# A top-k attention and token mixer on one core: the product's addend made by two-step instructions, scratch rows in turn, unread matmuls placed anew, and a refitted order

## The chip, the cores and the metric

The kernel runs on one core of a Trainium2 chip. The metric is the device time of one execution in microseconds (us). Five engines work side by side, each through its own list of instructions in order: PE (matrix products), DVE (maxima and small arithmetic), ACT (activations and copies out of PSUM), POOL (elementwise work), SP (which issues most transfers). The execution before takes 740.91 us (median of 3 runs, 740.88 to 741.44).

## What is computed

For 8 batches of 8 heads, 576 rows, head size 64: attention in which each row keeps only its 32 largest scores, then a token mixer and a channel mixer.

```python
scores = scale * np.matmul(q, k.transpose(0, 1, 3, 2))
kth = np.partition(scores, -top_k, axis=-1)[..., -top_k:-top_k + 1]
scores = np.where(scores >= kth, scores, -1000000000.0)
attn = softmax(scores)
x = (attn @ v).transpose(0, 2, 1, 3).reshape(B, S, H * D)
u = x + (np.maximum(x.transpose(0, 2, 1) @ w_tok1, 0.0) @ w_tok2).transpose(0, 2, 1)
out = u + np.maximum(u @ w_ch1, 0.0) @ w_ch2
```

## The kernel before

The 64 heads are 32 pairs. A pair's q, k and v are loaded and transposed, and its rows are taken 128 at a time. A *duo* is two such tiles (two heads of 128 rows, 576 scores each); there are 144 duos, in groups of one or two. For each duo:

- PE makes the scores (L552), and ACT copies them to `SX`, shifted and scaled (L367).
- DVE cuts each row into six pieces, takes the 8 largest of each (L589), and from these finds the place in the sorted row near which the 32nd value lies (L592 to L595). This gives an estimated threshold, `nh` (L684).
- ACT counts with a Sign how many scores are above the estimate (L606): the result goes to a scratch row `sg` that nobody reads, and the sum to `cnt`. From `cnt` small DVE instructions make `gs`, `ws` and `as` (all L684): whether to look above or below, and how far.
- POOL turns the scores into whole numbers that sort in the needed direction (L614, with a few fillers, L617), and DVE takes the 8 largest of the 584 (L623) into `tlo`. One of these is the exact threshold; `nt` (L684) is its negative.
- 100 duos (the *swapped* ones) then go through PE again: POOL makes a mask `U` (L632), PE adds it to the scores (L562, L568), and ACT takes the exponential into `Pm` (L637). The other 44 (the list `KEEP` and the duos that mix two pairs) do it on POOL: the addend `no` = 256 `gs` + `nt` is made on DVE (L703), POOL makes a byte mask `M` from it (L643) and multiplies the exponential `E` by it (L647).
- SP transposes `Pm` to `PT` by a transfer (L669); PE multiplies by v (L725), DVE divides by the sums into `Xb` (L739, L742).

After the four pairs of a batch come its mixers: L789 to L846 the token mixer, L911 and L897 the first channel product (`H`, and `Ht` for the last 64 rows of two batches), L863 and L868 the second, then ACT or DVE copies to `ob` (L881, L876) and SP stores.

All instructions are first put into a `Plan` with an engine, a duration and their dependences. The order in which they are issued is the string `ORDER`: two characters for each operation give its place. `Plan.run` walks through it, keeps for each engine the time at which it becomes free, and for each buffer (a `Buf`, a slot among equal tiles) when it can be taken. From these planned times follow two things: which slot or PSUM bank an operation gets, and where *unread matmuls* stand (`heat`, L1041): products of a constant that are written into a free bank and read by nobody, as many as fill eight tenths of the planned wait of PE. Nine stand at the start, 53 later.

The three copies that the small instructions write come from this helper; only the first is used, as a per-partition scalar on ACT or POOL:

```python
def thrice(x):
    return x.unsqueeze(1).to_broadcast([P, 3, x.shape[1]])
```

Of the kernel before, what the change touches and what calls it, by code (L numbers as in the profile page):

```python
# [8 lines left out]
P = 128  # L9
# [30 lines left out]
    "&1&J&Q&[&_'4&R&S'''-'7$-$0$?$S$]$@$e$A%#%+%-$;$i$<$=$|$>%&%.%>%T%E%R%S%_%`%g%s%p%q&C&e&m&p'0'2'1'3'8'q(0(2$M$U$X"  # L40
    "%$%2$b$c${%<%C%H%%%/%5%;%4%(%@%D%L$N$V$Z$a%)$g%0$}%6%I%W$_%3$~$y%7%*%?%J%Z%]%x%w%v%y&+&3&?&H&X&W&r&w&I&U&T&y'$'G"
    "'e'f'n'r(y'j(;(M(j({$j$t%,%1%A%=%a%G&'&*&6%b&-%f%d%c&%&4&7&;$W$s$z%K%~&$%'%^&,&:&=%8%X%V%[%B%M&(&2&@&B&]'.&`'*'@"
    "'<'D'g'l'h't(*'i'k'd(/(4(:(B(C(n(p(|(q(r(})E)r)w*2*4#3#2#5$.$/$C$B#R&M&L'6'(')'+',(@%O%P%e&G&9&E&>&b&f&l&q%U&A&0"
    "&5%h&D&k&u'%%N%Q%Y&h&s&z&n&i&~'>'A&#&c&<&/&8&j&{&}'E%|'H'Q'p'O'P()(~(#(+(=(?(A(^(d(>(D(E(g)$)&)7)C)D)I)U)u)L)Q)M"
    ")R)v%u%{&d&x'&&g'R'L'Y'b'x&F'='C&v&a'B'S'^($&Z&^&o'U'_&t'M'K'c'}(&&|'X'?'#']'J'a'z(((,(H(G(K(J(`(a(f)K(v(u)])c(t"
    ")P(s)e)m)o)x)y)}*V*Y)z)|*X*^*{'/';'I'Z'W'T'v'w(.(5(N'F'u(1(-(7'`(9(R(V's(](m(x)=)6)@)O){)N*0*8*>*H*O*Q*P*R*|+M+X"
    "+`':'N'y(U'|(Q(S(')#)*)-'V(h(T'[(P(%),)1)3'm'o'{(Y(3'~(Z(8(_)+)8(6)(([)%(W(O)0):)<)?)[)S)H)Z*7*;*?*J*M*L*b*i*K+$"
    "*N*y+:+=+P+Q+y+},)+N+{+~,(,x(F(I(X)_(b)a)^)`)d)p*$(c(e)h)>)4)g)k*#*)(o(w).)/)2);)j)5)q*'*,)')9)l)))b)i*%*(*/*1*T"
    "*]*S*[*z*g*r+(+)+&+>+F+'+S+%+W+c+g,$,%,+,-,w,2,3,K,p,y-9-F-H(L(i*I*U+z+|-Z-e(k(l*W*Z,,,7-h.?-i.G.A.F.B.H/Q/Y.Z/T"
    ".]/X.[.y/P/S181T171S151U1s1w1t1x2^2j2n3/3W3x4g5=5t6`5s5~6%<)'9'5-m)B)A)G)F.P&K(z&P*_*`+#*~,N)J)T*&***E*A*5*=*a*q"  # L50
    '*w)f)~*D*.)n*f*k*v+2)V)X*-*c*3*C*e*n*s+<+?*+*B*h*l*p*6*t+;+A+-+C+L+K+J+I+l,E+i+k,0,/,1,G,J,4,L,.,Q,U,X,[,s,t-$-/'
    "-j-4-8-6-T-k)W)Y*9*F*d*@*x*:+3+@+D*<*u*j*o*m*G+1+5+e+*+,+0+[+6+9+4+E+a+d+h+7+8+^+_+Z+Y+b+f+j+o,',8,6,&,T,S,],v,o"
    ',u-&-+-5-7-3-;-?-D-U-n.@.D/4-p-r.I.R/5+++.+B+s+V+w+n+u,:,<,D+U,A+t+x+m,>,B,I,P+G,^-1-#-L-A-J-q-o-s.2.9.<.a.t.v.u'
    '.w/6/[/d/h+/+H+T+r,@+],=,;,C,R,b+p,9+q+v,?,F,H,O,d,5,M,Y,_,Z,c,a,f,h,j,l,V,e,g,W,i,`,k,m,n-(-W-V-g-f.%.$./.J.Q.O'
    ".f.i.K.N.L.n/0/2/@/C/]/v04/A0'02060;,|-%-*-P-E---<-@-b-d-y-'-)-I-O-,-B-S-^-|-2-:-M-N-z-_-a-c.#.(.*-G-Q-v-`-u-R-x"
    ".'.,...V.W.C.E/'.s.|/=/>/:/G/I/?/</;/M/O/f0&0,0:0<1+0-0.0_0}1,1_1b1e,**}/7,q,r,},~0/)t,{)s.T.S.X.U1%-.-0-=->.&.5"
    '-C.1.8.l.p-K.h.7-}-{.c.k.o.{-X-Y-]-w.^.+.b.0.d.m.~-~.`.=.4.:.;.q.}/$.>/&/D/V/E/U/b0A/c/o0*0%0)0C0I0+000(0N0R0T0Z'
    "1&1N1i1m2b1(1)1'1*1/-[-t.).-.e.g.r.z/+/-/L.3/#/%.6._.j/K/N/`.Y.x/)/3/*/_/./^/g/l/t/(/1/H/,///J/n/q/x/}0512091319"
    '1:1>1K1M1L1Z1]1O1R1P1f1h1k1p1q262_2d1r282e2k2{/9/F/j/k0>/~0$/r0B0F0H/a/w/e/m/y/z/|0E0M/Z0V0^141^1C1H1`1a1Q1y1{1}'
    '2$27292;2f2m353I3M/R/W/i0D/p0#0L0Q0Y0a0i/s0K0U/{0c0[0n0x0{/u010@0k0J0j0b0h0o0r1<0?0s0q0v0p0G0|1=1A1I1u1W1V1X2U2#'  # L60
    '2,2g2h2<2r2t2i3(2:2y373=3R3S3w3{4=3Q3V3z4*4>07080O1;0P0X0W0y1?1D1F0S0t0f0z0e0m1B1G2)0=0]0`1E1c1g1[1z1~2(2-0d0g0w'
    "0l1@0u1d1|2/212l2a2`2]2u2w3'3*3,3+3;3>3)3-3.3@3D3G3T3U4)4:4?4&4'4O4X4e5>5z6.6[6a6^6d6v7;6}7T7Q7S7R7U8i8s8v8{8y8}"
    '9S9^8j8w9Q9W:*:>9R:=:+:U9U9]:,:T:d;%:c<&;2<$;1;C;F<%;>;E<#<.<3<p<t<r=-=Z@5=$=0=a=.=/=`Af/8-l2|1#0~11104$,z034h2~'
    "2}31305a161J1Y2'202.1j2+232@2L252=2D2E2O2H2S2V2X1l1n2&2?2F2A2I2N2P2W2Z2%2C2K2*2J242R2Y2v332z323O3Y3N3b3`3a3q3|3~"
    '4#40423}4(4%474F4J4N4R4S4o4p5k4U4V4T4W5l1o1v222M2>2G2q2x3<3K3[2B2T2Q2p2[2s3A3_3o2o3#3&3E3C3B393?3d3m3t3$3:3%383F'
    "3f3h3l3u4+4@4q494n5153595B5E5C5P5U5F5D5G5X5]5_5e5g6'6]6_5f6Q6c6q6r34363L3p3^4,3r434H4M4b3H3c4-3n3J464C4L4t3y5-5A"
# [1164 lines left out]
```

## Time and profile before

| what | value |
|---|---|
| median of 3 runs | 740.91 us |
| the profiled execution | 740.52 us |
| its span in the trace | 738.7 us |
| busy PE, DVE, ACT, POOL | 682.5, 675.4, 663.5, 637.4 us |
| mean granted clock of PE | 0.988 |

A row of the timeline has the start in us, the duration in us, the engine, the line, the operation, what it writes and reads, the count, and in brackets how long the engine was idle before it and for whom. Rows of groups end in busy us and mean ns of one, then the idle time ahead. Durations of successive DVE or ACT instructions overlap a little: what an instruction costs its engine is the time from its start to the next start. A window's row has its bounds and length, then busy us with counts for PE, PEld (weight loads), DVE, ACT and POOL, then the granted clock, the share of the transfer engines and GB/s.

### The profile page before, as it was taken

The page shows a single profiled execution, that of the slowest core. Times are in us where ns is not written, and L with a number is a line of the kernel's source. Part 1 is how long each engine was busy: PE and PEld are TensorE (multiplying, and loading weights), DVE is VectorE, ACT ScalarE, POOL GpSimd, SP SyncE. Part 2 cuts the span into 40 slices and gives each one's busy share as a digit, 9 for nine tenths or more (in the row PEclk, how much of TensorE's full clock was granted, in tenths as well). Part 3 has the DMA queues.
Part 4 walks back from the last instruction along what each step waited for, and adds up shares of the span by engine and source line. Part 5 has one row for each costly group of instructions (what it writes and reads, how often), then busy time and mean ns, then how long its engine had stood idle before and what let it go on. Part 6 is the DMA issues. An engine that isn't in the chain of part 4 may idle for free.

```text
span 738.7 us, 22205 instructions
## 1 busy us (share of the span) xinstructions
PE 682.5 (92%) x7478; PEld 379.1 (51%) x7478; DVE 675.4 (91%) x3768; ACT 663.5 (90%) x1134; POOL 637.4 (86%) x867
## 2 busy tenths in 40 slices
PE   7579789999998999999999999999989999999995
PEld 4235455455555555555555555554555655564652
DVE  7999999999999999999999999999999999996530
ACT  6979999999999999999899989999999999999341
POOL 3989999999889999989978999989999999999400
PEclk9879999999999999999999999999999999999998
DMA  5568798785856656874594486774676768644511
GB/s 130 99 128 150 124 164 152 144 142 83 182 94 139 134 123 97 162 145 81 106 169 111 88 135 123 175 131 95 108 148 121 151 103 121 133 74 100 129 45 61
DMA packets 286713, 90.42 MB, mean 122 GB/s; under 512 B 273024, under 2 KB 283136, under 8 KB 286592
## 3 DMA queue, kind: packets, MB, share of 16 engines
q1 hardware_dynamic: 282768, 84.97, 60.2%
q0 software_dynamic: 3024, 3.77, 3.6%
q8 instruction: 60, 0.98, 0.6%
q14 instruction: 61, 0.50, 0.2%
q10 hardware_dynamic: 800, 0.20, 0.1%
HBM read 35.85 MB, written 9.44 MB: 61 GB/s over the span
## 4 chain that ended last, share of the span: by engine, by line
DVE 49%; PE 18%; ACT 16%; POOL 10%; issue 3%; DMA 2%; SPq 0%; POOLq 0%; ACTq 0%; DVEq 0%
DVE cd L589 21%; DVE tlo L623 15%; ACT sg L606 6%; PE bank L863 4%; ACT SX L367 4%; POOL SX L614 4%; PE bank L911 3%; DVE cd L593 3%; PE bank L552 3%; POOL U L632 2%; ACT Pm L637 2%; DVE thi L595 2%; PE bank L568 2%; DVE m L592 2%; POOL Pm L647 2%
## 5 line engine op out<-in xcount | busy, mean ns | idle before, releaser
L589 DVE MAX8 cd<-SX 128x8 f32<-128x96 f32 x1728 | 342.1, 244 | 7.5 <-ACT SX L367 7.0
L614 POOL TENSOR_SCALAR SX<-SX,nh,gs 128x576 int32<-128x576 f32 x288 | 234.3, 821 | 11.6 <-DVE gs L684 3.6
L606 ACT ACTIVATE sg<-SX,nh 128x576 bf16<-128x576 f32 x288 | 223.6, 779 | 8.3 <-DVE nh L684 5.4
L623 DVE MAX8 tlo<-SX 128x8 uint32<-128x584 uint32 x288 | 218.3, 758 | 10.8 <-POOL SX L614 5.1
L552 PE MATMUL bank<-kT,qT 64*64 64x288 f32 x2304 | 175.0, 420 | 14.7 <-ACT SX L367 7.2
L632 POOL TENSOR_SCALAR U<-SX,nt,ws 128x576 uint8<-128x576 int32 x200 | 163.2, 825 | 20.9 <-DVE nt L684 8.7
L367 ACT ACTIVATE SX<-bank 128x1152 f32<-128x1152 f32 (+1 forms) x147 | 161.8, 1110 | 14.3 <-PE bank L552 12.3
L568 PE MATMUL bank<-kT,qT 64*128 64x288 f32 x800 | 124.4, 430 | 0.0
L552 PEld LDWEIGHTS bank<-kT,qT 64*64 64x64 f32 x2304 | 77.1, 134 | 91.6 <-ACT SX L367 22.3
L637 ACT ACTIVATE Pm<-bank 128x1152 bf16<-128x1152 f32 x100 | 112.8, 1131 | 8.9 <-PE bank L568 5.1
L647 POOL TENSOR_TENSOR Pm<-E,M 128x576 bf16<-128x576 bf16 x88 | 111.5, 1278 | 2.2 <-DMA PT<-Pm 0.5
L863 PE MATMUL bank<-wc2b,H 128*128 128x512 bf16 x384 | 90.9, 380 | 0.2
L911 PE MATMUL bank<-UT,wc1b 128*128 128x512 bf16 x380 | 89.6, 379 | 0.8 <-ACT SX L367 0.6
L568 PEld LDWEIGHTS bank<-kT,qT 64*128 64x128 f32 x800 | 69.1, 186 | 32.4 <-issue 22.4
L643 POOL TENSOR_SCALAR M<-SX,no,ws 128x576 int8<-128x576 int32 x88 | 72.2, 825 | 3.7 <-DVE no L703 1.9
L863 PEld LDWEIGHTS <-H 128*128 128x128 bf16 x384 | 34.6, 98 | 47.1 <-issue 12.8
L911 PEld LDWEIGHTS <-wc1b 128*128 128x128 bf16 x380 | 34.7, 98 | 45.9 <-issue 10.9
L606 ACT ACTIVATION_READ_ACCUMULATOR sg<-SX,nh 128x1 f32 x288 | 57.7, 200 | 0.0
L562 PE MATMUL bank<-U,identN 64*64 64x288 bf16 x800 | 45.1, 294 | 13.3 <-ACT SX L367 5.5
L725 PEld LDWEIGHTS <-PT 128*128 128x128 bf16 x1600 | 52.2, 98 | 9.0 <-issue 5.2
L600 ACT ACTIVATE E<-SX,lift 128x1152 bf16<-128x1152 f32 x44 | 55.4, 1260 | 0.1
L725 PE MATMUL bank<-vb,PT 128*128 128x65 bf16 x1600 | 54.4, 194 | 0.7 <-ACT SX L367 0.6
(124 smaller groups left out, 812.6 us busy)
## 6 DMA issues: line engine op xcount, KB each, us to landing
vL<-in_v_dram SPq DMA_DIRECT2D x64, 128.0 KB, 2.6
kL<-in_k_dram SPq DMA_DIRECT2D x63, 128.0 KB, 3.0
qL<-in_q_dram SPq DMA_DIRECT2D x62, 128.0 KB, 3.0
out_dram<-ob SPq DMA_DIRECT2D x14, 512.0 KB, 3.4
PT<-Pm SPq DMA_TRANSPOSE x143, 3.6
wc1b<-in_moe_w_ch_dram POOLq DMA_DIRECT2D x4, 384.0 KB, 4.8
...
```

The costliest lines, as they stand in the source:

```text
L367: nc.scalar.activation(out=dst, in_=src, func=AF.Copy, scale=GRID, bias=-LEVEL * GRID)
L552: nc.tensor.matmul(out=row(s1.t, h, lo, lo + HS, c, 64), lhsT=x["qT"].t[r, q0 : q0 + 64], rhs=x["kT"].t[r, lo : lo + HS], start=True, stop ...
L568: nc.tensor.matmul(out=row(s2.t, h, lo, lo + HS), lhsT=x["qT"].t[r, q0 : q0 + P], rhs=x["kT"].t[r, lo : lo + HS], start=False, stop=True)
L589: ss.append(plan.add("DVE", 0.06 + (bounds[a + 1] - bounds[a]) / 960, lambda a=a, h=h, cd=cd: nc.vector.max(cd.t[:, a, :], Sb.t[:, h, boun ...
L606: got.append(plan.add("ACT", 0.761, lambda i=i0 + 1 - h, h=h: nc.scalar.activation(out=sg[:, h, :], in_=Sb.t[:, h, 0:S], func=AF.Sign, sca ...
L614: xo.append(plan.add("POOL", 0.805, lambda i=i0 + 1 - h, h=h: nc.gpsimd.tensor_scalar(out=xi(Sb)[:, h, 0:S], in0=Sb.t[:, h, 0:S], scalar1= ...
L623: mxs.append(plan.add("DVE", 0.674, lambda i=i0 + 1 - h, h=h: nc.vector.max(tlo[:, at(i) - 7 : at(i) + 1], Sb.t[:, h, :].bitcast(u32)), [d ...
L632: us.append(plan.add("POOL", 0.805, lambda i=i0 + 1 - h, h=h: nc.gpsimd.tensor_scalar(out=byte(U.t[:, h, :], 1), in0=xi(Sb)[:, h, 0:S], sc ...
L637: oe = [plan.add("ACT", 1.013, lambda: nc.scalar.activation(out=Pm.t[:, :, 0:S], in_=pairs(s2.t), func=AF.Exp, scale=scale), [orr], use=[s ...
L647: oe.append(plan.add("POOL", 1.262, lambda h=h, M=M: nc.gpsimd.tensor_tensor(out=Pm.t[:, h, 0:S], in0=E.t[:, h, :], in1=M.t[:, :], op=ALU. ...
L863: nc.tensor.matmul(out=po, lhsT=H.t[:, fc, r0 : r0 + P], rhs=wc2b[:, fc, :], start=(fc == 0), stop=(rows is not None and fc == NF - 1))
L911: nc.tensor.matmul(out=o, lhsT=wc1b[:, cc, fc * P : (fc + 1) * P], rhs=UT.t[:, cc, :], start=(cc == 0), stop=(cc == (hi if whole else NC) ...
```

## The change

1. The addend `no` is made for each half of a duo by itself: 88 instructions in place of 44. Instead of one instruction with two tensor inputs over the whole group, each reads three copies of one value of `gs`, multiplies by the constant 256 and adds a value of `nt` that it gets as a pointer scalar. Each half's product on POOL waits for its own instruction.
2. The scratch row of the Sign is a slot of two that are taken in turn, and no longer the half of a fixed tile that belongs to the half of the duo.
3. Unread matmuls may go into a bank that the waiting operation itself is about to take, and are put in only where the planned start is before 80 us. 9 and 46 stand in place of 9 and 53.
4. Some planned durations are new, an SP transfer gets a surcharge when the transfers are behind, and `ORDER` is a new list with 44 more operations. (A line of it stands for all.)

```diff
 ORDER = (
-    "$I$r$o%k%o&Y&V(<+O+R,#.M/B1$###$#4#%#&#(#'#+#,#.#6#Q#*#)$(#M#K#S#O$L#-#/#0#7#1#?#8#=#<#C#A#@#E#H#J#9#;#:#F#B#D#G"
...
-    FAR = 0.09
-    LIT, FIRST = 0.5, 9
+    FAR, CLOG = 0.06, 0.25
+    WARM, LIT, FIRST = 80.0, 0.5, 9
...
-                bs = sorted((x[1], k) for k, x in enumerate(self.tags["ps"]) if x[2] and x[1] < st)
-                if bs:
+                own = [k for b in o.acq if b.tag == "ps" for k in b.slot]
+                bs = sorted((x[1], k) for k, x in enumerate(self.tags["ps"]) if (x[2] or k in own) and x[1] < st)
+                if bs and st < self.WARM:
...
-            o.end = free[o.eng] = st + o.dur
+            o.end = free[o.eng] = st + o.dur + (self.CLOG * max(0.0, dma_free - st - 2.0) if o.eng == "SP" else 0.0)
...
-    sg = sbt("sg", [P, 2, S], bf16)
+    sgs = slots("sg", 2, [P, S], bf16)
...
-                got.append(plan.add("ACT", 0.761, lambda i=i0 + 1 - h, h=h: nc.scalar.activation(
-                    out=sg[:, h, :], in_=Sb.t[:, h, 0:S], func=AF.Sign, scale=1.0, bias=nh.t[:, il - i : il - i + 1],
-                    accum_out=cnt[:, NT - 1 - i : NT - i]), [oh], use=[Sb, nh], lat=0.17))
+                sg = Buf("sg")
+                got.append(plan.add("ACT", 0.761, lambda i=i0 + 1 - h, h=h, sg=sg: nc.scalar.activation(
+                    out=sg.t[:, :], in_=Sb.t[:, h, 0:S], func=AF.Sign, scale=1.0, bias=nh.t[:, il - i : il - i + 1],
+                    accum_out=cnt[:, NT - 1 - i : NT - i]), [oh], acq=[sg], use=[Sb, nh], lat=0.17))
...
-                    ou = plan.add("POOL", 0.805, lambda i=i0 + 1 - h, h=h, M=M: nc.gpsimd.tensor_scalar(
-                        out=byte(M.t[:, :], 1).bitcast(i8), in0=xi(Sb)[:, h, 0:S], scalar1=no.t[:, il - i : il - i + 1],
+                    ou = plan.add("POOL", 0.83, lambda i=i0 + 1 - h, h=h, M=M: nc.gpsimd.tensor_scalar(
+                        out=byte(M.t[:, :], 1).bitcast(i8), in0=xi(Sb)[:, h, 0:S], scalar1=no.t[:, 3 * (il - i) : 3 * (il - i) + 1],
...
-                        [oo, ow], acq=[M], use=[Sb, no, ws])
+                        [oo[i0 + 1 - h], ow], acq=[M], use=[Sb, no, ws])
...
-            no = Buf("no")
-            oo = plan.add("DVE", 0.066 + 0.0035 * n, lambda: nc.vector.scalar_tensor_tensor(
-                out=no.t[:, 0 : 3 * n], in0=thrice(gs.t[:, 0:n]), scalar=256.0, in1=thrice(nt.t[:, 0:n]),
-                op0=ALU.mult, op1=ALU.add), [on], acq=[no], use=[gs, nt])
+            no, oo = Buf("no"), {}
+            for i in [d[0] + 1 - h for d in ds if not d[1] for h in (1, 0)]:
+                oo[i] = plan.add("DVE", 0.119, lambda i=i: nc.vector.tensor_scalar(
+                    out=no.t[:, 3 * (il - i) : 3 * (il - i) + 3], in0=thrice(gs.t[:, il - i : il - i + 1]), scalar1=256.0,
+                    scalar2=nt.t[:, il - i : il - i + 1], op0=ALU.mult, op1=ALU.add), [on],
+                    acq=[no] if len(oo) == 0 else [], use=[no, gs, nt])
```

The other edits are planned durations: transfers of q, k, v from 1.9 to 2.0, transposes from 1.36 to 1.4, stores from 0.65 to 0.7, weights' time on the transfer engines from 2.2 to 2.6, the scores' latency 0.29, and the judge at the end takes the two scratch rows by their new names.

The lists of instructions, at three places. First DVE in the middle of the program, around the 25th of the 44 addends, before (MAX of `cd` are the pieces of the next duos, `tlo` the 8 largest whole numbers of others):

```order
L684 TENSOR_SCALAR nt_163<-tlo 128x6
L589 MAX cd_103<-SX_92 128x8
L595 MAX thi<-cd_108 128x8
L589 MAX cd_107<-SX_92 128x8
L703 SCALAR_TENSOR_TENSOR no_167<-gs_135,nt_163 128x6
L684 TENSOR_SCALAR nh_117<-thi 128x12
L623 MAX tlo<-SX_97 128x8
```

and the same addend now:

```order
L590 MAX cd_108<-SX_93 128x8
L706 TENSOR_SCALAR no_167<-gs_136,nt_163 128x3
L596 MAX thi<-cd_107 128x8
L625 MAX tlo<-SX_98 128x8
L686 TENSOR_SCALAR nh_117<-thi 128x12
L706 TENSOR_SCALAR no_167<-gs_136,nt_163 128x3
L625 MAX tlo<-SX_98 128x8
```

One instruction has become two, with three instructions of other duos between them. Next, DVE where the last addend stands, ahead of the judge that looks through `cnt`, `tlo` and `thi` for bad values (L1003 to L1023), before:

```order
L684 TENSOR_SCALAR nt_166<-tlo 128x12
L703 SCALAR_TENSOR_TENSOR no_170<-gs_136,nt_166 128x12
L1003 MEMSET ones 128x1
L1004 TENSOR_SCALAR sg<-cnt 128x288
L1005 SCALAR_TENSOR_TENSOR sg<-sg,cnt 128x288
```

and now:

```order
L686 TENSOR_SCALAR nt_157<-tlo 128x12
L706 TENSOR_SCALAR no_170<-gs_135,nt_157 128x3 x2
L686 TENSOR_SCALAR ws_153<-cnt 128x12
L1007 MEMSET ones 128x1
L1008 TENSOR_SCALAR sg_172<-cnt 128x288
L1009 SCALAR_TENSOR_TENSOR sg_171<-sg_172,cnt 128x288
```

Here the two stand together, and a last `ws` has moved behind them. Last, PE at the end of the program, between the last product with `H` and the one with `Ht`, before:

```order
L863 LDWEIGHTS H_196
L863 MATMUL bank<-wc2b,H_196 128x512
L1041 LDWEIGHTS identB
L1041 MATMUL bank<-identB 128x512
...
L1041 MATMUL bank<-identB 128x512
L863 LDWEIGHTS Ht_197
L863 MATMUL bank<-wc2b,Ht_197 128x512
```

and now:

```order
L867 LDWEIGHTS H_197
L867 MATMUL bank<-wc2b,H_197 128x512
L867 LDWEIGHTS H_197
L867 MATMUL bank<-wc2b,H_197 128x512
L867 LDWEIGHTS Ht_198
L867 MATMUL bank<-wc2b,Ht_198 128x512
```

The six unread matmuls are gone, and the products follow each other.

More of the change, by code (lines that the diff above doesn't have):

```diff
@@ L42 @@
[L42 to L51, printed above, removed]
@@ L403, with weight @@
     wl = {}
-    def weight(key, at, lat, f, acq=(), dma=2.2):
+    def weight(key, at, lat, f, acq=(), dma=2.6):
         wl.setdefault(key, []).append(plan.add("POOL", 0.7, f, lat=lat, nb=at, acq=acq, dma=dma))
@@ L508, in front @@
             l1 = plan.add("SP", 1.9, rest, use=[qL], lat=3.1)
-            lv = plan.add("SP", 1.9, ld(vL, v, True), acq=[vL], dma=1.1, fly=1.2)
+            lv = plan.add("SP", 2.0, ld(vL, v, True), acq=[vL], dma=1.1, fly=1.2)
             o0 = plan.add("PE", 0.12, lambda: nc.tensor.transpose(
@@ L523, in front @@
             return dict(qT=qT, kT=kT, vb=vb, eq=eq, e0=[e0, ka], ek=kb, ov=cast(lv), PT=[])
-        lq = plan.add("SP", 1.9, ld(qL, q), acq=[qL], dma=1.66, fly=1.0)
-        lk = plan.add("SP", 1.9, ld(kL, k), acq=[kL], dma=1.66, fly=1.0)
-        lv = plan.add("SP", 1.9, ld(vL, v, True), acq=[vL], dma=1.1, fly=1.2)
+        lq = plan.add("SP", 2.0, ld(qL, q), acq=[qL], dma=1.66, fly=1.0)
+        lk = plan.add("SP", 2.0, ld(kL, k), acq=[kL], dma=1.66, fly=1.0)
+        lv = plan.add("SP", 2.0, ld(vL, v, True), acq=[vL], dma=1.1, fly=1.2)
         oq = plan.add("PE", 0.60, tr(pq, qL), [lq], acq=[pq, qT], use=[qL])
@@ L572, in scores @@
         om = plan.add("PE", 1.035, score, [x[w] for x, _ in sides for w in ("eq", "ek")],
-                      acq=[s1, Sb], use=ts, mode=(1, 1)) if i0 else None
+                      acq=[s1, Sb], use=ts, mode=(1, 1), lat=0.29) if i0 else None
         ev = [plan.add("ACT", 1.012, lambda: level(
@@ L668, in weights @@
             else:
-                od = [plan.add("SP", 1.36, lambda: nc.sync.dma_start_transpose(
-                    out=PTb.t[:, :, :], in_=Pm.t[:, :, :].rearrange("p h c -> p (h c)")), oe, acq=[PTb], use=[Pm], dma=1.84, fly=0.8)]
+                od = [plan.add("SP", 1.4, lambda: nc.sync.dma_start_transpose(
+                    out=PTb.t[:, :, :], in_=Pm.t[:, :, :].rearrange("p h c -> p (h c)")), oe, acq=[PTb], use=[Pm], dma=1.84, fly=0.6)]
             for x, _ in sides[: 2 - whole]:
@@ L978, in mlp_ops @@
             e = outs(H2, UT, i * P, h2, (ob, 0), i == 3, None if i == 3 else (ux, lambda i=i: turned_rows()[:, i : 16 : 4, :], ot))
-            plan.add("SP", 0.65, lambda ob=ob, i=i: nc.sync.dma_start(
+            plan.add("SP", 0.7, lambda ob=ob, i=i: nc.sync.dma_start(
                 out=out[b, 0:SM, :].rearrange("(p t) c -> p t c", t=4)[:, i, :], in_=ob.t[:, 0, :]), e, use=[ob], dma=1.0)
@@ L987, in st @@
                     out=out[b, 0:SM, :].rearrange("(p t) c -> p t c", t=4)[:, s0 : s0 + 2, :], in_=ob.t[:, :, :])
-            plan.add("SP", 0.65, st, es, use=[ob], dma=1.0)
+            plan.add("SP", 0.7, st, es, use=[ob], dma=1.0)
     for m in range(NPAIR // 2):
@@ L996 @@
     bad = sbt("bad", [P, 8], f32)
-    tmp = sg[:, 0, :].bitcast(f32)
-    ti = sg[:, 1, :].bitcast(i32)
+    tmp = sgs[0][:, :].bitcast(f32)
+    ti = sgs[1][:, :].bitcast(i32)
     ones = sbt("ones", [P, 1], f32)
```

205 lines of the change are left out of this document (108 added, 97 removed).

## The prediction, made before the result

> **What bounds the kernel now.** I read the busy shares and the chain of waits first, then windows of busy time by stage, then single instructions in the timeline. The page's line of engines and its chain:
>
> ```profile
> PE 682.5 (92%) x7478; PEld 379.1 (51%) x7478; DVE 675.4 (91%) x3768; ACT 663.5 (90%) x1134; POOL 637.4 (86%) x867
> ...
> DVE 49%; PE 18%; ACT 16%; POOL 10%; issue 3%; DMA 2%; SPq 0%; POOLq 0%; ACTq 0%; DVEq 0%
> ```
>
> Four engines are nearly full, but the chain that ended last lies on DVE for half of the span. The body and the ramp-down, by windows (microseconds busy on PE, PEld, DVE, ACT, POOL; then the granted clock):
>
> ```profile
> 20.00:660.00 640.00, 596.77 (x6740) 332.35 (x6733) 624.67 (x3552) 612.73 (x1042) 597.68 (x813) 0.99 0.69 127
> ...
> 660.00:680.00 20.00, 19.68 (x180) 10.38 (x178) 14.62 (x58) 19.38 (x40) 19.83 (x27) 1.00 0.40 91
> ```
>
> In the 640 us of the body DVE idles for 15.3 us only, ACT for 27.3, POOL for 42.3, PE for 43.2. So the body is worth what DVE's load is worth, with ACT close behind. From 660 on PE and POOL are full and DVE is not: there, PE's own instructions set the end.
>
> **Change 1: the product addend, 44 instructions become 88.** The view of the tile `nt` gives min/median/max in ns of the old instruction and, for comparison, of the ordinary small one:
>
> ```profile
> L703 DVE SCALAR_TENSOR_TENSOR no<-gs,nt x44: 148/304/1602, 25.0 to 683.5; 128x12 f32<-128x12 f32 x28, 128x6 f32<-128x6 f32 x16
> L684 DVE TENSOR_SCALAR nt<-tlo x80: 134/148/169, 23.9 to 683.2; 128x12 f32<-128x12 int32 x64, 128x6 f32<-128x6 int32 x16
> ```
>
> Same size, same engine: one never exceeds 169 ns, the other reaches 1602. The group row of the old one, then the DVE timeline where it is quick (303.01) and where it is worst (429.00), with an ordinary pair and a value load, and then POOL at the same moment:
>
> ```profile
> L703 DVE SCALAR_TENSOR_TENSOR no<-gs,nt 128x12 f32<-128x12 f32 (+1 forms) x44 | 19.2, 436 | 0.1
> ```
>
> ```profile
> 301.75 0.15 DVE L684 TENSOR_SCALAR nh<-thi 128x12 f32<-128x12 f32 x1
> 301.81 0.15 DVE L684 TENSOR_SCALAR nt<-tlo 128x12 f32<-128x12 int32 x1
> ...
> 303.01 0.15 DVE L703 SCALAR_TENSOR_TENSOR no<-gs,nt 128x12 f32<-128x12 f32 x1
> 303.09 0.25 DVE L589 MAX8 cd<-SX 128x8 f32<-128x96 f32 x1
> ...
> 304.61 0.07 DVE L593 MATCH_VALUE_LOAD cd<-m,cd 128x8 f32 x1
> 304.67 0.16 DVE L593 MATCH_REPLACE8 cd<-m,cd 128x18 f32<-128x18 f32 x1
> ...
> 429.00 1.60 DVE L703 SCALAR_TENSOR_TENSOR no<-gs,nt 128x6 f32<-128x6 f32 x1
> 430.53 0.15 DVE L684 TENSOR_SCALAR nh<-thi 128x12 f32<-128x12 f32 x1
> ```
>
> ```profile
> 429.08 0.82 POOL L632 TENSOR_SCALAR U<-SX,nt,ws 128x576 uint8<-128x576 int32 x1
> 429.87 0.73 POOL L464 TENSOR_SCALAR vb<-vL 128x640 bf16<-128x640 f32 x1
> 430.78 1.62 POOL L643 TENSOR_SCALAR M<-SX,no,ws 128x576 int8<-128x576 int32 x2 [0.18 <-DVE nh L684]
> ```
>
> The old instruction at 429.00 ends at 430.60, which is where POOL's unbroken run ends (429.87 + 0.73). I read this as DVE's instruction with two tensor inputs standing still until POOL lets it in. DVE is in order, so all its maxima queue behind it.
>
> Occupancy, start to next start: an unblocked one takes 0.08 (303.01 to 303.09) of its 0.15, so 0.07 overlap the next. All 44 hold DVE for 19.2 - 44 x 0.07 = 16.1 us, of which 44 x 0.08 = 3.5 is work and 12.6 is standing still.
>
> The new form has one tensor input and a pointer scalar in place of the second tensor. No DVE instruction of before has a pointer scalar with a plain tensor operation. Lower bound: the ordinary small instruction, 0.06 start to start (301.75 to 301.81), 88 x 0.06 = 5.3 us. Upper bound: blocked as the old one was, 16.1 / 44 = 0.366 each, 88 x 0.366 = 32.2 us. Nearest by mechanism is an ordinary one plus a load of a value per partition ahead of it, which the match operation shows as 0.06 (304.61 to 304.67): 0.12 each, 88 x 0.12 = 10.6 us. I take that: it saves DVE 16.1 - 10.6 = 5.5 us (bounds: saves 10.8, loses 16.1).
>
> One row bears on whether the new form is blocked. L684, one tensor input and three copies written, is never blocked (169 ns at most); by that row the sum is the 5.5 us saved. [...]
>
> **Change 2: the sign's scratch row.** Two adjacent signs on ACT that write the same half of `sg` wait for each other. Three adjacent pairs, the first one free, then the first and last held ones:
>
> ```profile
> 35.71 0.76 ACT L606 ACTIVATE sg<-SX,nh 128x576 bf16<-128x576 f32 x1
> 36.46 0.76 ACT L606 ACTIVATE sg<-SX,nh 128x576 bf16<-128x576 f32 x1
> ...
> 14.63 0.76 ACT L606 ACTIVATE sg<-SX,nh 128x576 bf16<-128x576 f32 x1
> 15.52 0.78 ACT L606 ACTIVATE sg<-SX,nh 128x576 bf16<-128x576 f32 x1
> ...
> 639.27 0.80 ACT L606 ACTIVATE sg<-SX,nh 128x576 bf16<-128x576 f32 x1
> 640.19 0.78 ACT L606 ACTIVATE sg<-SX,nh 128x576 bf16<-128x576 f32 x1
> ```
>
> Start to start 0.75 when free, 0.89 and 0.92 when held. 34 adjacent pairs lie at 0.88 to 0.97, so rows in turn free 34 x 0.14 = 4.8 us of ACT. Bounds: 0, should the pairs be held by something else, to 4.8. The value is the upper end, since only the shared half differs between the free and the held pairs.
>
> **What 1 and 2 give together in the body.** If DVE keeps its 15.3 us of idle time, the body shrinks by all of its 5.5; ACT, relieved of 4.8, follows, and PE and POOL have over 40 us idle. If only the parts on the chain count, it is 0.49 x 5.5 + 0.16 x 4.8 = 3.5. I take the middle, 4.5.
>
> **Change 3: unread matmuls.** None stand after 80 us of the planner's time any more. In the tail six stand ahead of the very last product (PE, then the ACT and DVE instructions that it needs):
>
> ```profile
> 723.33 2.76 PE L863 MATMUL bank<-wc2b,H 128*128 128x512 bf16 x12
> 725.93 1.46 PE L1041 MATMUL bank<-identB 128*128 128x512 bf16 x6
> 727.23 2.75 PE L863 MATMUL bank<-wc2b,Ht 128*128 128x512 bf16 x12
> ```
>
> ```profile
> 720.73 1.08 ACT L903 ACTIVATE Ht<-bank 128x512 bf16<-128x512 f32 x2 [0.30 <-PE bank L897]
> ...
> 723.32 0.69 DVE L876 TENSOR_TENSOR ob<-bank,SX 128x512 f32<-128x512 f32 x1 [3.68 <-PE bank L863]
> ```
>
> `Ht` is there at 721.8 and the DVE reader of an older bank is done at 724.0; PE has no idle time before 727.23. The six hold the end back by 727.23 - 725.93 = 1.3 us, and their removal gives 1.3, with nothing to take its place. Bounds 1.0 to 1.3.
>
> Early, they now may use the bank about to be taken, so they run while PE waits and no longer after it:
>
> ```profile
> 30.00:40.00 10.00, 3.28 (x34) 1.63 (x34) 10.00 (x71) 9.39 (x17) 9.65 (x16) 0.76 0.30 41
> 40.00:50.00 10.00, 9.51 (x65) 4.65 (x63) 9.72 (x51) 6.20 (x12) 9.76 (x14) 0.73 0.84 156
> 50.00:60.00 10.00, 8.41 (x125) 4.96 (x128) 9.40 (x65) 9.71 (x16) 7.58 (x11) 1.00 0.76 161
> ```
>
> ```profile
> 39.39 2.72 PE L1041 MATMUL bank<-identB 128*128 128x512 bf16 x6 [6.72 <-ACT SX L367]
> 42.04 2.20 PE L552 MATMUL bank<-kT,qT 64*64 64x288 f32 x16
> ```
>
> PE idles 6.72 us until a bank comes free and then spends 42.04 - 39.39 = 2.65 us on unread matmuls at a granted clock near 0.73, ahead of scores that ACT is waiting for (ACT 6.20 of 10). DVE lives on its stock meanwhile: it idles 0.28 + 0.60 = 0.9 us in 40 to 60. That 0.9 bounds the gain, 0 the other end (a loss of the same size if the sixteen that now stand there outlast the wait); I take 0.5.
>
> **Change 4: the list and its costs.** Every engine's order is new, SP's and POOL's queues among them, while counts of work stay. It can give back part of DVE's 15.3 us idle time or add to it; nothing in the trace of before prices an order that it does not hold. I take 0 with a third of the idle time, 5 us, to either side. The addend per half lets a POOL product start after its own half's addend; POOL's wait for `no` is inside its 42.3 idle us, so I price it at nothing, and at most at what DVE gains.
>
> **Sum.** 1.3 + 4.5 + 0.5 + 0 = 6.3 us less. The profiled execution took 740.52 us, span 738.7 with 1.8 around it; the runs' median is 740.91, so 0.4 above it. From the median: 734.6; the profiled execution by the same sum would be 734.2.
>
> **The rivals.**
> - *The new addend is blocked by POOL too, and there are twice as many.* For: POOL is busy 597.68 of 640, and the instruction still reads and writes beside it. Against: the small one-input instructions in the same trace are never blocked. Price: DVE +16.1; by the same middle of chain share (7.9) and whole (16.1), +12, less ACT's 0.8, the tail's 1.3 and 0.5 early: +9.4, 750. It decides from a mean of 16.1 / 88 = 0.18 us per new instruction on; up to there they hold DVE no longer than the old ones did. [...]
> - *Another engine holds the body.* DVE and ACT get faster and wait more, for POOL's whole numbers or PE's scores; POOL is full at 660 to 680 (19.83 of 20). Then the tail's 1.3 us is all: 739.6. Against: over 40 us idle on both in the body.
> - *The pointer costs nothing and the body follows DVE fully.* 10.8 + 1.3 + 0.9 = 13 us less: 728. For: 0.06 is what the ordinary ones take. Against: DVE is not alone on the chain.
>
> **How the numbers follow.** Forecast 0.56, blocked 0.16, another engine 0.14, pointer free 0.14. Range 727 to 743: the low end is the free pointer with 1 us more from the list; the high end is the case of another engine with 3.4 us lost to the list, and leaves the blocked case out, which is most of the 2 in 10. About 0.2% (1.5 us) is what a measurement of this kernel can tell from no change. Faster by more: 0.56 + 0.14 + 0.06 of the other-engine case = 0.76; within: 0.08; slower: 0.16. The likeliest case's own range is 729 to 740.
>
> **What would show it.** The addend's group: 88 instructions with a maximum near 0.2 us and DVE occupancy near 10.6 us; a median of 0.3 and maxima over 0.8 would mean blocked. Adjacent signs all near 0.76 start to start. No unread matmul after 80 us, and the last product directly behind the one before it. In 30 to 50 us a granted clock near 1 and ACT above 6.20 of 10. DVE still over 97% busy from 20 to 650. If DVE's idle time in the body grows by as much as its load falls, the body term is wrong; if POOL or ACT waits for something that the old order had early, the list term is.

## The result, and the profile after

| | before | after |
|---|---|---|
| median of the runs | 740.91 us (first 3); 741.04 beside the changed kernel | 750.61 us (748.80 to 751.00) |
| ratio | | 1.0123, 95% interval 1.0106 to 1.0141 |
| the profiled execution; its span | 740.52; 738.7 us | 750.24; 748.5 us |
| mean granted clock of PE | 0.988 | 0.985 |

The kernel became 1.2% slower. The forecast was 734.6, and the direction was wrong. The rival with the blocked addend had given 750; that it comes so near is in part luck, as point 3 below shows. The page's line of engines and its chain, after:

```profile
PE 680.3 (91%) x7405; PEld 380.7 (51%) x7471; DVE 685.7 (92%) x3812; ACT 660.9 (88%) x1134; POOL 637.6 (85%) x867
...
DVE 68%; ACT 11%; PE 7%; POOL 6%; issue 3%; DMA 2%; SPq 0%; POOLq 0%; ACTq 0%; DVEq 0%
```

DVE is the one engine of the four that is busy for clearly longer (685.7 us, from 675.4), and its share of the chain went from 49% to 68%. The tile view of the addend and of the ordinary small instruction (min/median/max in ns), and then three groups: POOL's masks before, POOL's masks after, and the addend:

```profile
L706 DVE TENSOR_SCALAR no<-gs,nt x88: 204/302/2123, 23.2 to 694.5; 128x3 f32<-128x3 f32 x88
...
L686 DVE TENSOR_SCALAR nt<-tlo x80: 100/148/168, 22.7 to 692.3; 128x12 f32<-128x12 int32 x64, 128x6 f32<-128x6 int32 x16
```

```profile
L643 POOL TENSOR_SCALAR M<-SX,no,ws 128x576 int8<-128x576 int32 x88 | 72.2, 825 | 3.7 <-DVE no L703 1.9 <-DVE thi L595 0.4 <-DVE m L592 0.4
...
L645 POOL TENSOR_SCALAR M<-SX,no,ws 128x576 int8<-128x576 int32 x88 | 72.5, 825 | 10.4 <-DVE no L706 7.9 <-DVE m L593 0.6 <-DVE ws L686 0.3
...
L706 DVE TENSOR_SCALAR no<-gs,nt 128x3 f32<-128x3 f32 x88 | 38.7, 449 | 0.2
```

The new addend has the old one's long tail: a mean of 449 ns and a maximum of 2123, where the ordinary small instruction ends at 168. There are twice as many. From each one's start to the next DVE start (or its own end, whichever is earlier) they hold DVE for 31.6 us, and the 44 old ones held it for 15.7 by the same count. POOL's masks `M`, which waited 3.7 us before, now wait 10.4, most of it for the addend. One of the longest, first on DVE and then on POOL:

```profile
433.78 0.24 DVE L590 MAX8 cd<-SX 128x8 f32<-128x96 f32 x1
433.94 2.08 DVE L706 TENSOR_SCALAR no<-gs,nt 128x3 f32<-128x3 f32 x1
435.93 0.18 DVE L596 MAX8 thi<-cd 128x8 f32<-128x36 f32 x1
```

```profile
433.56 2.44 POOL L616 TENSOR_SCALAR SX<-SX,nh,gs 128x576 int32<-128x576 f32 x3
436.19 0.82 POOL L645 TENSOR_SCALAR M<-SX,no,ws 128x576 int8<-128x576 int32 x1 [0.20 <-DVE thi L596]
```

The addend of three values starts at 433.94 and ends at 436.02, and the three POOL instructions that run without a gap end at 436.00. It is the picture that the old instruction gave at 429.00 in the kernel before.

Most waits are shorter. Of the 88 new addends 37 take over 400 ns, and each of these 37 ends within 60 ns of the end of a POOL instruction (18 of 18 among the old ones; the stretches within 60 ns of such an end are 14% of the span). Only 16 of the 37 end where POOL then pauses for over 30 ns. The other 21 got in between two POOL instructions that follow each other without a pause, and 30 of the 37 got in at the first end of a POOL instruction that they met.

Where on the way the time was lost is seen from windows that end with the last search of a row (L623 before, L625 after). Before, then after:

```profile
0.00:683.25 683.25, 635.73 (x7068) 352.75 (x7069) 657.87 (x3724) 647.70 (x1105) 629.03 (x859) 0.99 0.67 126
```

```profile
0.00:692.30 692.30, 634.80 (x7000) 354.83 (x7061) 666.80 (x3765) 643.37 (x1103) 628.90 (x859) 0.99 0.65 124
...
20.00:660.00 640.00, 586.36 (x6548) 327.46 (x6597) 625.00 (x3534) 601.93 (x1026) 588.70 (x799) 0.99 0.66 125
...
660.00:680.00 20.00, 19.27 (x243) 11.92 (x243) 19.79 (x112) 19.33 (x40) 19.10 (x24) 1.00 0.50 105
```

The searches end 9.05 us later. DVE is busy 8.9 us longer until then, and its idle time is the same (25.4 and 25.5 us). So all of it is DVE's own load. Of the addends' 15.9 us more, 13.8 lie in this stretch and the last two addends behind it take the rest. DVE's other work takes 4.9 less. ACT and POOL wait more, for they do no more work (ACT 4.3 us less) in a longer time. In 660 to 680 DVE was busy for 14.62 of 20 us before and is now full. The tail behind the searches takes 55.45 us before and 56.2 after.

### The profile page after: what moved, and what is told of

It is laid out like the page before. It is cut to its first block, busy times and chain, and to the rows that moved or that the text cites. A ratio compares the mean times of both kernels' runs of the same rounds, so it can differ in the third digit from the quotient of the medians.

```text
span 748.5 us, 22183 instructions
## 1 busy us (share of the span) xinstructions
PE 680.3 (91%) x7405; PEld 380.7 (51%) x7471; DVE 685.7 (92%) x3812; ACT 660.9 (88%) x1134; POOL 637.6 (85%) x867
## 4 chain that ended last, share of the span: by engine, by line
DVE 68%; ACT 11%; PE 7%; POOL 6%; issue 3%; DMA 2%; SPq 0%; POOLq 0%; ACTq 0%; DVEq 0%
DVE cd L590 28%; DVE tlo L625 20%; DVE cd L594 4%; DVE no L706 4%; ACT sg L608 4%; DVE thi L596 3%; ACT SX L368 3%; DVE m L593 3%; POOL SX L616 2%; PE bank L867 2%; DVE Xb L746 2%; DMA PT<-Pm 2%; POOL U L634 2%; ACT Pm L639 1%; ACT H L961 1%
## 5 line engine op out<-in xcount | busy, mean ns | idle before, releaser
L625 DVE MAX8 tlo<-SX 128x8 uint32<-128x584 uint32 x288 | 218.8, 760 | 11.1 <-POOL SX L619 4.8
L569 PE MATMUL bank<-kT,qT 64*128 64x288 f32 x800 | 127.2, 437 | 0.0
L867 PE MATMUL bank<-wc2b,H 128*128 128x512 bf16 x359 | 88.8, 382 | 2.1 <-issue 1.2
L915 PE MATMUL bank<-UT,wc1b 128*128 128x512 bf16 x357 | 86.9, 379 | 2.3 <-ACT Pm L639 0.5
L645 POOL TENSOR_SCALAR M<-SX,no,ws 128x576 int8<-128x576 int32 x88 | 72.5, 825 | 10.4 <-DVE no L706 7.9
```

Of the source, the lines that this page charges most:

```text
L569: nc.tensor.matmul(out=row(s2.t, h, lo, lo + HS), lhsT=x["qT"].t[r, q0 : q0 + P], rhs=x["kT"].t[r, lo : lo + HS], start=False, stop=True)
L625: mxs.append(plan.add("DVE", 0.674, lambda i=i0 + 1 - h, h=h: nc.vector.max(tlo[:, at(i) - 7 : at(i) + 1], Sb.t[:, h, :].bitcast(u32)), [d ...
L867: nc.tensor.matmul(out=po, lhsT=H.t[:, fc, r0 : r0 + P], rhs=wc2b[:, fc, :], start=(fc == 0), stop=(rows is not None and fc == NF - 1))
L915: nc.tensor.matmul(out=o, lhsT=wc1b[:, cc, fc * P : (fc + 1) * P], rhs=UT.t[:, cc, :], start=(cc == 0), stop=(cc == (hi if whole else NC) ...
```

## Experiments

Three theories stood at first. **A, the shape:** an instruction with one tensor input is held by POOL when its input and output have the same outer count, here three and three; unequal counts, such as three rows read and one run of six written, free it. (The outer count is the number of rows of a tile's access; where there is but one row, the number of its values.) **B, the pointer scalar:** the second read of a value per partition is what is held, whatever the shape. **C, the order:** the refitted list and not the addend costs the time. Each kernel was compared with the kernel before on the same chip; the ratios are against that one. "Held" below is DVE's time in the addends, counted as above; "searches end" is where the last search of a row ends in the profiled run (that of the addend alone, 760.45 us, lies 5 above its median; the others are within 2.1). Both come from one profiled execution of each kernel.

| kernel | ratio, 95% interval | addends: count, held us | searches end |
|---|---|---|---|
| before | 1 | 44, 15.7 | 683.25 |
| the change | 1.0123, 1.0106 to 1.0141 | 88, 31.6 | 692.3 |
| addend alone, old order | 1.0176, 1.0156 to 1.0196 | 88, 31.8 | 697.3 |
| order, rows and unread matmuls alone | 1.0039, 1.0023 to 1.0054 | 44, 24.3 | 686.9 |
| wide addend | 0.9984, 0.9962 to 1.0005 | 88, 10.9 | 675.4 |
| wide addend and 88 plain ones of three | 1.0197, 1.0169 to 1.0225 | 88, 11.4; plain 88, 25.1 | 697.0 |
| wide addend in rows of two | 1.0116, 1.0090 to 1.0141 | 88, 33.5 | 698.0 |
| wide addend, old order | 1.0077, 1.0055 to 1.0098 | 88, 11.0 | 682.4 |
| wide addend, judge later | 0.9889, 0.9869 to 0.9908 | 88, 10.9 | 676.6 |
| wide addend, old order, judge later | 1.0008, 0.9992 to 1.0024 | 88, 11.1 | 682.5 |
| the change, judge later | 1.0109, 1.0083 to 1.0136 | 88, 32.4 | 693.7 |
| before, judge later | 1.0058, 1.0038 to 1.0079 | 44, 18.6 | 687.0 |
| scratch rows alone | 0.9995, 0.9982 to 1.0008 | 44, 16.5 | 683.2 |
| before without late unread matmuls | 1.0021, 1.0005 to 1.0038 | 44, 21.1 | 687.7 |

### The addend alone, in the old order

The kernel before with the new addends in the place of the old one, one behind the other:

```diff
-            oo = plan.add(..., lambda: nc.vector.scalar_tensor_tensor(out=no.t[:, 0 : 3 * n], ...), [on], ...)
+            def apart():
+                for i in [d[0] + 1 - h for d in ds if not d[1] for h in (1, 0)]:
+                    nc.vector.tensor_scalar(
+                        out=no.t[:, 3 * (il - i) : 3 * (il - i) + 3], in0=thrice(gs.t[:, il - i : il - i + 1]),
+                        scalar1=256.0, scalar2=nt.t[:, il - i : il - i + 1], op0=ALU.mult, op1=ALU.add)
+            oo = plan.add(..., apart, [on], ...)
```

> The kernel before with the new addend alone: at the old instruction's place the two or four new ones follow each other, all else as before. Theory A: they are held as in the changed kernel; the second of a group finds POOL running again only if POOL got in between, so occupancy is 20 to 32 us against 16.1, and the time 743 to 753. Theory B says the same. Theory C: no slower than 742.

755.41 us against 741.47, ratio 1.0176. The tile's view:

```profile
L705 DVE TENSOR_SCALAR no<-gs,nt x88: 209/248/2581, 25.8 to 700.1; 128x3 f32<-128x3 f32 x88
```

The addend alone adds 16.1 us to DVE's load in the profiled execution and 13 to 14 to the time (13.0 by the ratio, 13.9 by the medians); 755.41 lies above the 753 that A and B had as their upper end. It is enough to explain the result, and the change as a whole is less slow than this part of it.

### The order alone

The changed kernel with the old instruction, given out by `once` for the whole group, at the place of the first of its halves:

```diff
-                oo[i] = plan.add("DVE", 0.119, lambda i=i: nc.vector.tensor_scalar(...), ...)
+                oo[i] = plan.add("DVE", 0.119, once, ...)
```

> The changed kernel (its order, scratch rows and unread matmuls) with the old addend instruction with two tensor inputs, once per group, at the place of the first of the group's new ones. Theory A: the 44 hold DVE for about 16 us as in the kernel before, and order, rows and unread matmuls together then give 0 to 7 us: 734 to 741. Theory C: the time stays near 748 to 751 although the addend is the old one. Theory B says the same as A here.

744.25 us, ratio 1.0039, between what the theories had given. The tile's view says why:

```profile
L706 DVE SCALAR_TENSOR_TENSOR no<-gs,nt x44: 96/459/3342, 24.1 to 687.1; 128x12 f32<-128x12 f32 x28, 128x6 f32<-128x6 f32 x16
```

The same 44 instructions hold DVE for 24.3 us and not 15.7: 24 of them take over 400 ns and not 18, and the longest 3342 ns and not 1602. With 8.6 us more of DVE in the addends the kernel loses only 2.9, so order, rows and unread matmuls seem to gain some of it back. C is refuted as the main cause.

### The wide addend

The changed kernel with the pointer scalar kept, but with two neighbouring values read three times and six written; the tile `no` is twice as wide, and POOL reads the first of the six:

```diff
-                    out=no.t[:, 3 * (il - i) : 3 * (il - i) + 3], in0=thrice(gs.t[:, il - i : il - i + 1]), scalar1=256.0,
+                    out=no.t[:, 6 * (il - i) : 6 * (il - i) + 6], in0=thrice(gs.t[:, il - i : il - i + 2]), scalar1=256.0,
```

> The changed kernel with one edit: each addend instruction reads three rows of two values and writes a run of six (odd against even, unequal), with the pointer scalar as it is. Theory A (the shape of three in and three out makes DVE wait for POOL): no instruction is held, each takes 0.12 us from start to next start, 88 x 0.12 = 10.6 us in place of 31.6, maximum below 0.3 us, and the time falls by half to all of 21 us, to between 730 and 740. Theory B (the pointer scalar makes it wait, whatever the shape): occupancy stays near 31.6 us, maxima above 1 us, time stays 748 to 752. Theory C (the new order is what is slow): occupancy falls to 10.6 us, but the time stays above 744.

740.03 us, ratio 0.9984, at the upper end of what A had given. The tile's view, and DVE at the end of the searches:

```profile
L706 DVE TENSOR_SCALAR no<-gs,nt x88: 166/204/221, 22.5 to 675.8; 128x6 f32<-128x6 f32 x88
```

```profile
675.65 0.35 DVE L706 TENSOR_SCALAR no<-gs,nt 128x6 f32<-128x6 f32 x2
675.92 0.16 DVE L686 TENSOR_SCALAR ws<-cnt 128x12 f32<-128x12 f32 x1
676.00 7.52 DVE L1008 TENSOR_SCALAR sg<-cnt 128x288 int32<-128x288 f32 x1
...
689.41 0.82 DVE L746 TENSOR_TENSOR Xb<-bank,rds 128x640 bf16<-128x640 f32 x1
```

No addend takes over 221 ns now; 88 hold DVE for 10.9 us, 0.12 each, with a pointer scalar in every one. B is refuted. But of the 17 us by which the searches end earlier than in the change only 10 reach the end. The judge's first instruction, 288 values read and 288 written, stands for 7.52 us where it took 0.30 in the change, and PE waits for the division queued behind it:

```profile
690.29 0.69 PE L563 MATMUL bank<-U,identN 64*64 64x288 bf16 x7 [5.19 <-DVE Xb L746]
```

POOL's run ends 0.17 us ahead of that instruction (683.35 and 683.52):

```profile
680.79 2.56 POOL L649 TENSOR_TENSOR Pm<-E,M 128x576 bf16<-128x576 bf16 x2
```

In the change the last two addends had waited for POOL's pause in its place, 2.24 us. The waiting has moved to another instruction with one input and equal counts.

### Plain instructions of three beside the wide addend

The wide one, with an instruction of three values with constants only ahead of each addend; its output is read by nobody:

```diff
+                    nc.vector.tensor_scalar(
+                        out=spare3[:, 4 * (i % 4) : 4 * (i % 4) + 3], in0=thrice(gs.t[:, il - i : il - i + 1]),
+                        scalar1=256.0, scalar2=1.0, op0=ALU.mult, op1=ALU.add)
```

> The first experiment's kernel (addend of 3 x 2 in, 6 out) with one more DVE instruction ahead of each of the 88 addends: three rows of one value in, three out, times a constant plus a constant, no pointer scalar, into a scratch tile that nobody reads. Theory A (the shape): these 88 are held as the changed kernel's addends were, with maxima above 0.8 us and 20 to 32 us in all, and the time is 750 or more. Theory B2 (shape and pointer scalar together): they cost the ordinary 0.06 to 0.07 us, 88 x 0.07 = 6 us in all, none above 0.25 us, and the time is 741 to 746.

755.87 us, ratio 1.0197. The two groups, then both instructions at one place, and POOL there:

```profile
L708 DVE TENSOR_SCALAR spare<-gs 128x3 f32<-128x3 f32 x88 | 33.1, 376 | 0.0
L711 DVE TENSOR_SCALAR no<-gs,nt 128x6 f32<-128x6 f32 x88 | 18.2, 208 | 0.0
```

```profile
436.72 2.08 DVE L708 TENSOR_SCALAR spare<-gs 128x3 f32<-128x3 f32 x1
438.71 0.20 DVE L711 TENSOR_SCALAR no<-gs,nt 128x6 f32<-128x6 f32 x1
438.84 0.18 DVE L597 MAX8 thi<-cd 128x8 f32<-128x36 f32 x1
```

```profile
436.36 2.43 POOL L617 TENSOR_SCALAR SX<-SX,nh,gs 128x576 int32<-128x576 f32 x3
```

The plain one without a pointer stands still until POOL's three are done (436.36 + 2.43 = 438.79, against 436.72 + 2.08 = 438.80). The one with a pointer behind it takes 0.13 to the next start. This settles A against B within one kernel.

### The wide addend in rows of two

What was left is whether the wide form is free because its outer counts differ or because it has six values. The six are written as three pairs a pitch of four apart, so that input and output both count three by two:

```diff
-    out=no.t[:, 6 * (il - i) : 6 * (il - i) + 6], in0=thrice(gs.t[:, il - i : il - i + 2]), ...
+    out=no.t[:, 12 * (il - i) : 12 * (il - i) + 12].rearrange("p (a b) -> p a b", b=4)[:, :, 0:2], in0=thrice(...), ...
```

> The changed kernel with the addend that reads 3 x 2 values and writes six, as in the wide one, but the six are laid out as three pairs a pitch of four apart, so that input and output both count 3 in their outer step; what is computed, the pointer scalar and the number of instructions stay. Theory A (what decides is that the outer counts of the one input and of the output are odd and equal): the addends are held again, 88 with about 0.36 us each, 30 to 33 us of VectorE in all, longest over 1 us, and the time is 748 to 753. Rival D (the wide form was free because it handles six values, or even ones): about 11 us in all, none over 0.3 us, and the time is 738 to 742 as the wide one's.

753.13 us against 743.80 on this chip, ratio 1.0116. The tile's view:

```profile
L706 DVE TENSOR_SCALAR no<-gs,nt x88: 201/338/2143, 24.1 to 700.2; 128x6 f32<-128x6 f32 x88
```

The same values, the same number of them, the same pointer scalar: of the instruction only the layout of what is written differs from the wide one, and the maxima go from 221 to 2143 ns, the held time from 10.9 to 33.5 us. A holds for the counts that were run, and D is refuted. Held were three and three (31.6 and 33.5 us for 88) and the judge's 288 and 288 (7.52 us in the wide one), and three against six was not (221 ns at most in the wide one). That equal counts have to be odd is not shown: of those held, three is odd and 288 even.

### The wide addend with the judge moved

The judge's first eight instructions go behind the division of the last pair but one, the rest ahead of the sums:

```diff
+                    if p == NPAIR - 2:
+                        judge1()
...
     def judge():
+        pass
+
+    def judge1():
         nc.vector.memset(ones[:, :], 1.0)
...
+    def judge2():
         nc.vector.tensor_copy(out=tmp, in_=tli[:, 7 : NT + 7])
...
     def sums():
+        judge2()
```

> The first experiment's kernel with the judge at the end cut in two and put behind the division of the last pair but one and ahead of the last sums, where POOL has finished. In the first experiment its first instruction (288 values, one input) stood 7.46 us at POOL, and PE idled 5.19 us for the division queued behind it. Theory A: nothing of it is held, PE's idle time there goes, 4 to 6.5 us less than the first experiment: 733.5 to 736. Rival: POOL's last products set the tail anyway, and the time stays within 2 us of 740.

732.88 us against 741.24, ratio 0.9889 (0.9869 to 0.9908): faster than both kernels, and a little below the 733.5 to 736 of theory A. DVE's rows at the end of the searches:

```profile
676.79 0.35 DVE L706 TENSOR_SCALAR no<-gs,nt 128x6 f32<-128x6 f32 x2
677.05 0.15 DVE L686 TENSOR_SCALAR ws<-cnt 128x12 f32<-128x12 f32 x1
684.63 0.22 DVE L743 RECIPROCAL rds<-bank 128x10 f32<-128x10 f32 x1 [7.43 <-PE bank L729]
684.89 0.82 DVE L747 TENSOR_TENSOR Xb<-bank,rds 128x640 bf16<-128x640 f32 x1
685.64 0.30 DVE L1016 TENSOR_SCALAR sg<-cnt 128x288 int32<-128x288 f32 x1
```

DVE is now idle for 7.43 us ahead of the division and waits for PE, where PE had waited 5.19 for DVE; the judge's first instruction takes 0.30, which I put down to POOL's unbroken run being over (by the page POOL is busy for 4 tenths of 676.6 to 694.9). Against the wide one this gives 7.2 us.

### The same move without the wide addend

Does the move by itself give seven microseconds? It was made in the changed kernel and in the kernel before.

> The changed kernel with its own addend of three values, and the judge cut in two and moved as in the version at 732.9 us. There the addend stays held. Theory A: the body still ends some 16 us later than with the wide addend, and since the judge wasn't held in the changed kernel (0.30 us for its first instruction; TensorE waited 1.1 us for the division behind it) it gains 1 to 3 us: 747.5 to 749.5. Rival F (moving the judge is worth seven microseconds by itself, whatever the addend): 742 to 744.

> The kernel before with nothing changed but the judge, cut in two and moved. In the kernel before TensorE waited 0.22 us for the division behind the judge, whose first instruction took 1.0 us. Theory A: within 1 us of the kernel before, 740 to 741.5. Rival F (moving the judge is worth seven microseconds by itself): 733 to 735.

The changed kernel: ratio 1.0109, within what was measured without the move (1.0123), so F (742 to 744) is refuted there. The addends hold DVE for 32.4 us. The kernel before became slower, 1.0058, which neither A nor F had expected. PE's row in its tail:

```profile
716.98 1.86 PE L916 MATMUL bank<-UT,wc1b 128*128 128x512 bf16 x4 [2.89 <-DVE H L954]
```

In the old order the judge's second half now stands between two of the additions `H` that PE's next products need. That is 2.9 of the 4.3 us. Four of its five executions also had a mean granted clock of 0.979 to 0.983, where the kernel before beside it had 0.982 to 0.990. The held time of the old addends is 2.8 us larger as well (18.6), in a body whose instructions stand in the same order. Whether that is the chip, the phase or the single profiled execution is open.

### The wide addend in the old order

The kernel before with the wide form (as in the addend alone, with six written), and then also with the judge moved.

> The kernel before (its order, scratch rows, unread matmuls) with the addend as in the first experiment: 88 of 3 x 2 in, 6 out, two or four in a row. DVE is held for 88 x 0.12 = 10.6 us in place of 16.1. If DVE's load passes through as in the run with the addend alone (15.8 us more load gave 13.9 us), 4.8 us less: 736 to 738. If the time stays within 1 us, the body is held by another engine once DVE is below the load of before.

> The kernel before with the wide addend in its own old order (746.2 us), and the judge cut in two and moved behind the division of the last pair but one. Theory A (the wide addend frees VectorE in the body, and the judge's first instruction stood 7.3 us in the tail in place of it): the held time goes, 738 to 740 us, and the difference to the kernel before is what the old order's body gives, 1 to 3 us. Rival E (the old order's tail has a limit of its own, TensorE's): 743 to 746.

746.22 us, ratio 1.0077, and then 744.2, ratio 1.0008. The first was to be faster and is slower; its rows at the end of the searches and the window up to there:

```profile
682.58 0.35 DVE L705 TENSOR_SCALAR no<-gs,nt 128x6 f32<-128x6 f32 x2
682.85 7.32 DVE L1008 TENSOR_SCALAR sg<-cnt 128x288 int32<-128x288 f32 x1
```

```profile
0.00:682.40 682.40, 634.99 (x7066) 351.93 (x7067) 653.85 (x3767) 647.25 (x1105) 628.68 (x859) 0.99 0.66 126
```

The judge is held as in the wide one, and the move takes 5.1 us away (1.0077 to 1.0008), although PE then waits 2.90 us behind the judge's second half as above. The result lies between what A (738 to 740 against 741.2, so 0.996 to 0.998) and rival E (743 to 746, so 1.002 to 1.006) had given. The body is the other half: DVE is busy 4.0 us less than in the kernel before, but the searches end only 0.85 earlier, since DVE's idle time grew from 25.4 to 28.6. In the new order the same addend lets them end at 675.4 to 676.6, with 26.0 and 27.7 us of idle time. I read this as other engines holding the body in the old order once DVE is relieved, and less so in the new one; one profiled execution of each kernel stands behind it (with the judge moved, the old order ended them at 682.5, with 28.7).

### The scratch rows alone

```diff
-                    out=sg[:, h, :], in_=Sb.t[:, h, 0:S], func=AF.Sign, ...
+                    out=sg[:, next_row(), :], in_=Sb.t[:, h, 0:S], func=AF.Sign, ...
```

> The kernel before with the sign's scratch rows in turn alone. Theory A: no adjacent pair of signs is held (34 at 0.88 to 0.97 us before, then all at 0.75 to 0.81), ACT is relieved of 4.8 us, and the time falls by 0.8 to 2 us, to 739 to 740.3. The other answer, that DVE alone sets the body and ACT's relief is only idle time: 740.7 to 741.4.

740.94 us, ratio 0.9995. The pair that was held at 639 in the kernel before:

```profile
639.24 0.80 ACT L612 ACTIVATE sg<-SX,nh 128x576 bf16<-128x576 f32 x1
...
640.01 0.78 ACT L612 ACTIVATE sg<-SX,nh 128x576 bf16<-128x576 f32 x1
```

Start to start 0.77 where it was 0.92; of 97 adjacent pairs one is held and not 34, and their mean falls from 826 to 774 ns. ACT's 5 us are freed as predicted, and the time does not move by more than the interval (at most 1.3 us less).

### The late unread matmuls alone

The kernel before without the unread matmuls that the planner places after 80 us, six in the tail among them. It has 33 fewer, and not 7 fewer as the change, which puts others in before 80 us:

```diff
+                        if st < 80.0:
                             order.append(lambda c=x[0], early=early: self.heat(c, early))
```

> The kernel before without its unread matmuls whose planned start is after 80 us; banks and order as before. The six ahead of the last product go, and some single ones in the body. Theory: the last product starts 1.3 us earlier, the time falls by 1.0 to 1.5 us. Rival: the last product then waits for its bank or a transfer as long as before, 0 us; or the granted clock falls in the body without them, slower.

743.47 us, ratio 1.0021 (1.0005 to 1.0038): a little slower, where 1.0 to 1.5 us less was expected. In the tail the last product now follows directly on the one ahead:

```profile
729.98 2.76 PE L864 MATMUL bank<-wc2b,H 128*128 128x512 bf16 x12
732.58 2.75 PE L864 MATMUL bank<-wc2b,Ht 128*128 128x512 bf16 x12
```

Here it starts 2.60 us after the one ahead, and 3.90 in the kernel before, so the predicted 1.3 are there, and the body took them back. Two things differ in the body. In the profiled execution the old addends hold DVE for 21.1 us and not 15.7, and the judge starts at 690.44 and not 683.55. And the granted clock is lower: seven of the twelve executions had a mean of 0.978 to 0.983 and took 743.4 to 745.8 us, the other five had 0.985 to 0.989 and took 740.2 to 741.9, and the kernel before beside it had 0.984 to 0.991. That is the rival of a falling clock. It fits these executions, and the profiled one (0.983, 745.51 us) is one of the seven, but how much is the clock and how much the addends isn't separated.

## Why the prediction was wrong, point by point

1. **The price of the new addend, 0.12 us each and 10.6 in all, is the step that failed.** The 88 hold DVE for 31.6 us, close to the rival's 32.2. The step went over from an ordinary small instruction that is never held (169 ns at most) to a new form by adding a load of a value. The row it leaned on, L684, reads three rows and writes one run of six or twelve; the new one reads three and writes three. What this difference is worth showed only in the runs: from the wide addend to the one in rows of two, where only the layout of what is written changes, the held time goes from 10.9 to 33.5 us. The wide addend shows that 0.12 is right for an instruction with a pointer scalar that is not held.
2. **The reading that the old instruction waits for POOL was right**, and so was the point from which the rival decides: a mean of 0.18 us per new instruction was named, 0.36 was measured. That it waits for the end of POOL's unbroken run, as the row at 429.00 suggested, is right for a part only: of the 18 old addends over 400 ns, 11 ended at a pause of POOL and 7 between two POOL instructions without one.
3. **What the body makes of DVE's load.** For the blocked case the text took the middle between the chain's share and the whole, 12 of 16.1 us. The addend alone lost 13 to 14 of 16.1. The rival's 750 met the result in part by luck: its 12 was one or two us too small, and for the rest of the change it took off 2.6 us, where point 5 has 3.9. For less load, in the old order only 0.85 of 4.0 us came through up to the end of the searches, which would be the rival of another engine that holds the body.
4. **The scratch rows** freed ACT's 4.8 us (5 measured), and gave nothing in the time that could be told. The 0.8 us that the lower end counted for it lies within the interval of that run (0.9982 to 1.0008), so the run doesn't decide about it.
5. **The list, priced at 0 with 5 to either side, seems to be worth 4 us or more.** The change beats its own addend by 0.5% (1.0123 against 1.0176, 3.9 us), and with the wide addend and the judge moved the new order beats the old by 1.2% (0.9889 against 1.0008, 8.8 us, of which 2.9 is PE's wait behind the judge's second half). These differences hold the rows and the unread matmuls too; the rows alone gave nothing that could be told, so I put most of it down to the order, which no run isolates.
6. **The tail.** In the change the last product follows directly on the one ahead:

```profile
733.62 2.76 PE L867 MATMUL bank<-wc2b,H 128*128 128x512 bf16 x12
736.22 2.75 PE L867 MATMUL bank<-wc2b,Ht 128*128 128x512 bf16 x12
```

The last starts 2.60 us after the one ahead, and 3.90 before, so the term of 1.3 was right. Behind it 0.8 us were lost again: from the last product's start to the end of the span it is 11.4 us before and 12.2 after, for which I have no cause.
7. **Early.** Windows of the change:

```profile
30.00:40.00 10.00, 9.13 (x54) 3.92 (x52) 10.00 (x53) 8.33 (x16) 9.79 (x16) 0.68 0.82 131
40.00:50.00 10.00, 9.47 (x91) 5.23 (x90) 10.00 (x63) 8.29 (x13) 9.22 (x12) 1.00 0.50 98
```

ACT in 40 to 50 rose from 6.20 to 8.29, and the clock is 1.00 there (0.73 before), but 0.68 in 30 to 40 (0.76). The predicted signs are there from 40 on only. DVE's idle time in 40 to 60 fell from 0.9 to 0.25, but DVE carries more load here, so this shows no gain of its own.
8. **What no rival had:** relieved of the held addends the kernel did not reach 734.6 but 740.03, because the judge's first instruction was held in their place. Only with that moved does it stand at 732.88.
